# Where a slot's fill products stand: first half filled up to a third of the phase in place of a quarter

## The chip, the core and the metric

The kernel runs on one core of one Trainium2 chip. Times are device microseconds (us) of that core, from the start to the end of one execution. TensorE (PE, matmuls and their weight loads), VectorE (DVE), ScalarE (ACT), GpSimd (POOL) and SyncE (SP, which issues the DMAs here) each work through their own instructions in order and wait for each other through semaphores. Matmuls write to PSUM banks; ACT and DVE read them from there.

## What is computed

The reference works on 2048 tokens of 512 channels. `x` is layer-normed to `xn`. Branch A is causal attention with a window of 256 keys and 32 heads of 16 channels; branch B layer-norms `xn` again, and applies a two-layer MLP of 1792 hidden channels with tanh-GELU. The result is

```
s = attention(xn @ wqkv, window 256) @ wo        # 32 heads of 16
g = silu(gelu(layernorm(xn) @ w1 + b1) @ w2 + b2)
out = x + s * g
```

The kernel splits each float32 operand into a high and a low part and adds three matmuls (high·high, high·low, low·high) where the reference has one product.

## The kernel before, in words

**Stages.** A first stage loads and normalises `x` and projects the first heads (to about 62 us). The attention stage runs to about 447 us. The rest (447 to 764 us) is the MLP and the output projection.

**The attention stage** goes through 128 blocks, t = 0 to 127: eight groups n of four heads, with 16 blocks of 128 keys each. Within a group the heads are handled as two pairs, p = 1 and p = 0. One block, in the order in which PE gets its work (the loop is `for t in range(-16, end + 1)`, line 819):

1. `prob_block(p=1)` (line 548): two score matmuls into the tile `stb`, then an exponential on ACT from `stb` into a tile `pt`, then two mask operations on POOL.
2. `max_block` (line 496): four score matmuls into `xy` for the row maxima of the block 12 ahead (`LEAD`). DVE puts masked values from `zo` into `xy` (COPY_PREDICATED) and reduces `xy` to the maxima `mt` (TENSOR_REDUCE).
3. `fill_in(t, 0)` (line 812): the **first half's fill products**.
4. What `plan` holds for this block (casts, weight splits, DMAs).
5. `prob_block(p=0)`: again two score matmuls into `stb`, and the exponential. There is one `stb` tile, so these matmuls wait until the exponential of step 1 has read it; likewise step 1 of the next block waits for the exponential of this step.
6. `fill_in(t, 1)`: the **second half's fill products**.
7. `first_scores` (line 487): four matmuls into `zo` for the next block's maxima; they follow DVE's COPY_PREDICATED, which reads `zo`.
8. `pv_step` (line 569): up to 24 small matmuls of `pt` with the values `vt` into another part of `zo`, which ACT copies to `oraw`.

For t from 116 on there are no maxima left, and step 1 writes to `xy` instead of `stb`.

**The fill products** are work of other stages that is put between the attention's matmuls: query/key projections of later heads (`pair_qk`, 12 products to a phase), value projections (`pair_v`, 24), and hidden layers of the MLP (`pair_h`, 12). `tandem(t0, t1, one, two)` (line 440) makes two of them at once: each unit is a pair of matmuls on the lower and the upper 64 rows of the array, writing to the two banks `fb`. It has two phases (in the second, the operands change rows), n units each. `places` deals the n units of a phase over the blocks (slots) of that phase in even shares, and then splits each block's share between the first and the second half of the block; `ahead` (line 455) is the number in the first half. The second phase keeps up to `most` = n // 4 units for the first half of block t1. At t1 the two banks are copied out, one by ACT and one by DVE; then the high part is cast on ACT, the low part subtracted on POOL, and both are sent by DMA into the slots from which later blocks read queries and keys.

All instructions but the DMAs of an early part keep the order in which the program issues them.

Of the kernel before, what the change touches and what calls it, by code (L numbers as in the profile page):

```python
# [50 lines left out]
def mixer_kernel(ctx, tc, x, wqk, wv, wo, w1, b1, w2, b2, out):  # L51
# [25 lines left out]
    def load(pool, tag, src, name, shape=(P, 512)):  # L77
        t = pool.tile(list(shape), F32, tag=tag, name=name)
        nc.sync.dma_start(t, src)
        return t  # L80
# [359 lines left out]
    def tandem(t0, t1, one, two, mid=None, back=None):  # L440

        n = one[0]
        lo, hi = slice(0, 64), slice(64, P)
        mid = mid or max(1, (t0 + t1 + 1) // 2)
        most = n // 4

        def places(slots, last):

            last = min(most, n // (len(slots) + 1)) if last else 0
            cuts = [(n - last) * k // len(slots) for k in range(len(slots) + 1)]
            out = []
            for t, a, b in zip(slots, cuts, cuts[1:]):
                ahead = min(b - a, max(most, (b - a + 1) // 2))
                out += [(t, 0)] * ahead + [(t, 1)] * (b - a - ahead)
            return out + [(t1, 0)] * last

        first, second = places(range(t0, mid), False), places(range(back or mid, t1), True)
        for phase, where in enumerate((first, second)):  # L460
            for i in range(n):
                flags = dict(start=(phase == 0 and i == 0), stop=(phase == 1 and i == n - 1), skip_group_check=True)
                def unit(i=i, phase=phase, flags=flags):
                    made = ((two if phase == 0 else one)[1](fb[1 - phase], i, hi, **flags),
                            (one if phase == 0 else two)[1](fb[phase], i, lo, **flags))
                    if phase == 1 and i == 0:
                        for r in made:
                            tc.add_manual_dep(r.ins, outs["copy"].ins.name, ORDER, reason="the banks change rows")
                fills.setdefault(where[i], []).append((unit, ()))
        fills.setdefault((t1, int(t1 in BEHIND)), []).append((one[2], (fb[0], t1, nc.scalar.copy)))  # L470
        fills[t1, 0].append((two[2], (fb[1], t1, nc.vector.tensor_copy)))
# [203 lines left out]
    ahead = load(pp, "pt", x[512: 640, :], "x_1_0")  # L675
# [28 lines left out]
    n, raw = raws["qk"]  # L704
# [600 lines left out]
```

## Time and profile before

| | us |
|---|---|
| median of 3 runs | 765.21 (765.13 to 765.72) |
| the profiled execution | 765.6 |
| its span, first to last instruction | 763.9 |
| blocks 0 to 115 of the attention stage | 62 to about 409 |
| blocks 116 to 127 and the end of that stage | about 409 to 447 |
| MLP and output projection | 447 to 764 |

The profile is of one execution. The 1.7 us between its time and its span lie outside the first and last instruction. In a timeline view a row is a run of equal instructions: start, length of the run, engine, operation, output<-inputs, shape, count, and in brackets the idle time before the first one with what ended it. Matmul ends are modelled, so a matmul row can reach over the start of the next; the starts are what is compared below. PEld are weight loads, which run beside the matmuls.

### The profile page before, as it was taken

To read this page: it belongs to the slowest core of one execution; us is meant where nothing else is said; L and a number is where in the kernel's file an instruction comes from. 1 tells how busy PE (TensorE), PEld (TensorE's weight loads), DVE (VectorE), ACT (ScalarE), POOL (GpSimd) and SP (SyncE) were. 2 spreads that over 40 slices of the span, in tenths; PEclk is the share of its full clock that TensorE was granted. 3 is DMA by queue.
4 is the path that set the end of the run, shared out by engine and by line. 5 is a ranking of instruction groups with operands and counts; after the bars stand their busy time and mean duration, and the time that the engine had idled before them with its cause. 6 is when DMAs were issued, how large, how long until landed. Compare 5 with 4: busy or idle time off the path is not lost.

```text
span 763.9 us, 18757 instructions
## 1 busy us (share of the span) xinstructions
PE 748.9 (98%) x7408; PEld 587.6 (77%) x7408; DVE 511.2 (67%) x781; ACT 440.3 (58%) x746; POOL 300.4 (39%) x644
## 2 busy tenths in 40 slices
PE   8999999999999999999999999999999999999997
PEld 7886766777778887677776678888888888888886
DVE  7886766767766677887764447764657675676743
ACT  7756766767666666777877755444645553442001
POOL 6414657767566554867776800030101100001102
PEclk9999999999999999999999999999999999999999
DMA  8633345756555535555644283541202322244611
GB/s 282 187 78 83 79 121 145 195 148 185 140 136 137 136 87 156 134 153 132 173 153 152 61 276 129 186 156 42 83 28 89 104 85 85 80 150 133 215 54 55
DMA packets 56951, 99.40 MB, mean 130 GB/s; under 512 B 11104, under 2 KB 11360, under 8 KB 56864
## 3 DMA queue, kind: packets, MB, share of 16 engines
q1 hardware_dynamic: 56864, 98.21, 44.9%
q8 instruction: 58, 0.95, 0.5%
q14 instruction: 29, 0.24, 0.1%
HBM read 51.39 MB, written 29.62 MB: 106 GB/s over the span
## 4 chain that ended last, share of the span: by engine, by line
PE 87%; ACT 5%; DVE 3%; DMA 2%; issue 2%; POOL 0%; SPq 0%; ACTq 0%; DVEq 0%
PE acc L43 20%; PE fb L43 16%; PE zo L43 13%; PE stb L43 10%; PE p L43 9%; PE s L43 6%; PE h L43 6%; ACT pt L43 4%; PE xy L43 4%; PE pv L43 3%; DMA qk<-qk 2%; DVE xy L43 1%; PE yt L43 1%; DMA x<-in_x_dram 1%; DVE mt L43 1%
## 5 line engine op out<-in xcount | busy, mean ns | idle before, releaser
L43 POOL TENSOR_SCALAR_AFFINE_SELECT pt<-pt 128x256 f32<-128x256 f32 x480 | 194.8, 430 | 146.1 <-ACT pt L43 144.7
L43 ACT ACTIVATE pt<-stb 128x768 f32<-128x768 f32 (+1 forms) x244 | 188.6, 773 | 50.4 <-PE stb L43 39.6
L43 DVE TENSOR_REDUCE mt<-xy 128x4 f32<-128x1024 f32 (+1 forms) x128 | 152.6, 1192 | 4.4
L43 DVE COPY_PREDICATED xy<-upper,zo 128x512 f32<-128x512 int32 x112 | 77.9, 695 | 84.4 <-PE xy L43 77.1
L43 PE MATMUL fb<-xnT,wqb 64*128 64x512 f32 (+1 forms) x684 | 112.9, 398 | 0.2
L43 PE MATMUL stb<-qk 64*128 64x384 f32 (+1 forms) x488 | 103.1, 418 | 4.4 <-ACT pt L43 1.1
L43 POOL TENSOR_TENSOR xo<-xo,gated 128x512 f32<-128x512 f32 x15 | 20.3, 1356 | 216.6 <-DVE gated L43 213.1
L43 PE MATMUL zo<-pt,vt 128*17 128x128 f32 x2880 | 103.7, 275 | 0.1
L43 PE MATMUL acc<-w,gh 128*128 128x512 f32 x320 | 98.9, 390 | 0.0
L43 PEld LDWEIGHTS stb<-qk 64*128 64x128 f32 x488 | 45.5, 183 | 68.7 <-ACT pt L43 57.7
L43 PEld LDWEIGHTS zo<-pt,vt 128*17 128x17 f32 x2880 | 67.5, 97 | 15.7 <-issue 7.0
L43 PEld LDWEIGHTS fb<-xnT,wqb 64*128 64x128 f32 (+1 forms) x684 | 63.8, 185 | 7.8 <-DVE pjr L43 1.1
L43 PEld LDWEIGHTS acc<-w,gh 128*128 128x128 f32 x320 | 59.8, 188 | 12.1
L43 ACT COPY oraw<-zo 128x128 f32<-128x128 f32 x128 | 34.3, 268 | 56.7 <-PE zo L43 53.5
L43 PE MATMUL acc<-w,gl 128*128 128x512 f32 x160 | 62.4, 390 | 0.0
L43 PE MATMUL xy<-qk 64*128 64x256 f32 (+2 forms) x536 | 58.0, 290 | 0.3 <-DVE mt L43 0.2
L43 PEld LDWEIGHTS xy<-qk 64*128 64x128 f32 x536 | 47.0, 185 | 6.4 <-issue 2.8
L43 ACT ACTIVATE gated<-acc 128x512 f32<-128x512 f32 x16 | 8.7, 596 | 64.5 <-DVE acc L43 64.5
L43 PEld LDWEIGHTS zo<-qk 64*128 64x128 f32 x448 | 39.2, 185 | 7.8 <-issue 1.4
L43 PE MATMUL s<-wos,ohl 128*128 128x512 f32 (+1 forms) x204 | 44.7, 377 | 0.0
L43 PEld LDWEIGHTS s<-wos,ohl 128*128 128x128 f32 x204 | 36.6, 188 | 7.0
L43 ACT COPY p<-p 128x512 f32<-128x512 f32 x21 | 12.3, 585 | 49.5 <-PE p L43 42.0
(195 smaller groups left out, 1245.1 us busy)
## 6 DMA issues: line engine op xcount, KB each, us to landing
qk<-sh SPq DMA_DIRECT2D x128, 128.0 KB
qk<-pjr SPq DMA_DIRECT2D x64, 128.0 KB
oT_d<-oraw SPq DMA_DIRECT2D x32, 256.0 KB
w_d<-in_w_dram SPq DMA_DIRECT2D x14, 512.0 KB
x<-in_x_dram SPq DMA_DIRECT2D x16, 256.0 KB
or<-oT_d SPq DMA_DIRECT2D x16, 256.0 KB
w<-rden_d SPq DMA_DIRECT2D x16, 256.0 KB
xo<-in_x_dram SPq DMA_DIRECT2D x16, 256.0 KB
```

The lines of the kernel that those rows point to most:

```text
L43: r = issue(*args, **kwargs)
```

## The change

One line of `places` changes. In each block of a tandem phase, the number of units in the first half was the larger of a quarter of the phase and half of the block's share, and is now the larger of a third of the phase and half of the share, never more than the share.

```diff
@@ tandem, places
             for t, a, b in zip(slots, cuts, cuts[1:]):
-                ahead = min(b - a, max(most, (b - a + 1) // 2))
+                ahead = min(b - a, max(n // 3, (b - a + 1) // 2))
                 out += [(t, 0)] * ahead + [(t, 1)] * (b - a - ahead)
             return out + [(t1, 0)] * last
```

With n = 12 the first half holds up to 4 units in place of 3, and with n = 24 up to 8 in place of 6. Shares are 4, 5 or 6 units with n = 12 and 8, 9 or 12 with n = 24, so (first half, second half) goes from (3, 1), (3, 2), (3, 3) to (4, 0), (4, 1), (4, 2), and from (6, 2), (6, 3), (6, 6) to (8, 0), (8, 1), (8, 4). That is 99 blocks, of which 91 lie before t = 116; each moves one unit with n = 12 and two with n = 24, 116 units in all. The number `last` of units at t1 still follows `most` and stays. A moved unit now stands before the second score matmuls of its block on PE, where it stood after them; no instruction is added or removed, and the order of the other engines' instructions and of the DMAs stays.

## Prediction

> **What bounds the kernel now.** I read the page's busy times first, then the stretches, then the table of waits, then PE's own timeline in single blocks.
>
> ```profile
> PE 748.9 (98%) x7408; PEld 587.6 (77%) x7408; DVE 511.2 (67%) x781; ACT 440.3 (58%) x746; POOL 300.4 (39%) x644
> ```
> ```profile
> 62.19:408.00 345.81, 339.88 (x5027) 250.49 (x5028) 250.89 (x312) 243.35 (x418) 225.58 (x521) 1.00 0.54 138
> 447.00:764.00 317.00, 312.29 (x1413) 258.96 (x1411) 194.46 (x350) 126.11 (x209) 26.13 (x20) 1.00 0.34 112
> ```
> ```profile
> PEld stb L43 <- ACT pt L43: 57.7, 172, 0.5
> ```
>
> The second fence has stretches: length, then busy time of PE, PEld, DVE, ACT and POOL, then granted clock, DMA share and GB/s. In the changed stage (62 to 408 us) PE counts as busy for 339.9 of 345.8 us, so 5.9 us of idle at most. The waits tell more: weight loads for `stb` stood 172 times, 57.7 us in all, until ACT's exponential had read `stb`. A row of matmuls has modelled ends, so a hole in front of a waiting matmul can be covered by the row before it. Starts can't hide it.
>
> ```profile
> 187.37 0.44 PE L43 MATMUL stb<-qk 64*128 64x384 f32 x2
> 187.65 0.40 PE L43 MATMUL xy<-qk 64*128 64x256 f32 x4
> 187.89 0.87 PE L43 MATMUL fb<-xnT,wqb 64*128 64x512 f32 x6
> 188.80 0.44 PE L43 MATMUL stb<-qk 64*128 64x384 f32 x2
> 189.08 0.33 PE L43 MATMUL zo<-qk 64*128 64x128 f32 x4
> ...
> 190.15 0.44 PE L43 MATMUL stb<-qk 64*128 64x384 f32 x2
> 190.43 0.40 PE L43 MATMUL xy<-qk 64*128 64x256 f32 x4
> 190.76 0.97 PE L43 MATMUL fb<-xnT,wqb 64*128 64x512 f32 x6
> ...
> 193.14 0.44 PE L43 MATMUL stb<-qk 64*128 64x384 f32 x2
> 193.42 0.40 PE L43 MATMUL xy<-qk 64*128 64x256 f32 x4
> 193.65 0.87 PE L43 MATMUL fb<-xnT,wqb 64*128 64x512 f32 x6
> 194.57 0.44 PE L43 MATMUL stb<-qk 64*128 64x384 f32 x2
> 194.85 0.40 PE L43 MATMUL fb<-xnT,wqb 64*128 64x512 f32 x2
> 195.09 0.33 PE L43 MATMUL zo<-qk 64*128 64x128 f32 x4
> ...
> 196.13 0.45 PE L43 MATMUL stb<-qk 64*128 64x384 f32 x2
> ```
> ```profile
> 202.54 0.86 PE L43 MATMUL fb<-xnT,wqb 64*128 64x512 f32 x6
> 203.24 0.39 PE L43 MATMUL stb<-qk 64*128 64x256 f32 x2
> ```
> ```profile
> 187.94 0.81 ACT L43 ACTIVATE pt<-stb 128x768 f32<-128x768 f32 x1 [0.16 <-PE stb L43]
> 189.29 0.81 ACT L43 ACTIVATE pt<-stb 128x768 f32<-128x768 f32 x1 [0.54 <-PE stb L43]
> ```
>
> The block at 193.14 is a usual (3, 1) block. A pair costs 0.23 (194.85 to 195.09). From `stb` to `stb` its first half should last 0.28 + 0.23 + three pairs: in a block near a group's end, where the exponential is short, three pairs pass in 0.70 (202.54 to 203.24), so 1.21. It lasts 1.43 (193.14 to 194.57), as the three pairs take 0.92. **There is a hole of 0.22 us in the first half.** ACT's rows say why: the exponential starts 0.57 after its matmuls (187.37 to 187.94), takes 0.81, and the next `stb` follows 0.05 later. The second half has the same chain, a little shorter (0.49 + 0.81 + 0.05 = 1.35): the block at 187.37 is a t1 block (3, 0), and its second half lasts just that (188.80 to 190.15). With one pair in it a second half lasts 1.56 (194.57 to 196.13): there PE is the bound, by 0.21.
>
> So a block's time is the longer of PE and the exponential's chain, in each half apart; now the first half waits for ACT and the second works PE beyond it.
>
> [...] Read by busy time, 5.9 us is all there is to win here.
>
> **The change, part by part.** Nothing is added or taken away; PE's order alone changes, by 116 pairs in 99 blocks. What a move is worth depends on the block; I went through the starts of all 91 changed blocks before t = 116 (the first at 71.89, the last at 406.25):
>
> ```profile
> 71.89 0.44 PE L43 MATMUL stb<-qk 64*128 64x384 f32 x2
> ```
> ```profile
> 406.25 0.45 PE L43 MATMUL stb<-qk 64*128 64x384 f32 x2 [0.16 <-ACT pt L43]
> ```
>
> For each I took: new first half = old + 0.23 a moved pair (0.118 for a value pair) − the hole in its pairs' time; new second half = old − the same, but not under the chain's 1.35.
>
> - *47 blocks of 512-wide pairs with a full effect.* In (3, 1) the fourth pair fills the hole: 0.28 + 0.23 + 0.92 = 1.43 to 1.44, and the second half falls from 1.56 to 1.35. (3, 2) and (3, 3) keep pairs in the second half and save the whole 0.23. Gains of 0.17 to 0.23, 0.203 on average: **−9.56 us**.
> - *11 value blocks with a full effect.* Twelve matmuls take 0.91 (232.20 to 233.11), six without a hole 0.36 (233.39 to 233.75), so 0.12 a pair and a hole of 0.20. Eight pairs take 0.94; two pairs leave the second half: 0.195 each, **−2.14 us**.
>
> ```profile
> 232.20 0.92 PE L43 MATMUL fb<-wva,xnT 64*128 64x256 f32 x12
> 233.11 0.44 PE L43 MATMUL stb<-qk 64*128 64x384 f32 x2
> 233.39 0.52 PE L43 MATMUL fb<-wva,xnT 64*128 64x256 f32 x6
> 233.75 0.34 PE L43 MATMUL zo<-qk 64*128 64x128 f32 x4
> ```
>
> - *14 blocks with half an effect.* After a t1 block the first pair waits for DVE's copy of the bank (190.43 to 190.76 is 0.33, not 0.23), so part of the hole is before the pairs; or the second half soon meets 1.35; or the block follows a group's end. **−1.42 us** (0.10 each).
> - *19 blocks with none.* Near a group's end the exponentials are short and no hole is there (202.54 to 203.24): the pair costs in one half what it saves in the other. In a group's first blocks `pv_step` is short, and the second half stands at the chain already, pair or no pair:
>
> ```profile
> 212.01 0.45 PE L43 MATMUL stb<-qk 64*128 64x384 f32 x2
> 212.29 0.40 PE L43 MATMUL fb<-xnT,wqb 64*128 64x512 f32 x2
> ...
> 213.35 0.44 PE L43 MATMUL stb<-qk 64*128 64x384 f32 x2 [0.16 <-ACT pt L43]
> ```
>
> There the fourth pair saves nothing (212.01 to 213.35 is 1.34 with a pair inside) and costs up to 0.1: **+0.38 us**.
>
> - *8 blocks from t = 116 on*: maxima are done, `xy` and `stb` alternate, and the pairs run without a hole; moving one changes nothing: 0. Bounds: a gain of 0.2 each would need a hole that isn't there, a loss the same, ±1.6.
>
> Sum of the blocks: −9.56 − 2.14 − 1.42 + 0.38 = −12.74.
>
> **What comes back.** *A DMA.* In block 11 PE stood for the DMAs that bring in a chunk of queries and keys of the second group:
>
> ```profile
> 93.47 1.18 SPq L43 DMA_DIRECT2D qk<-pjr  x2
> ```
> ```profile
> 98.47 0.44 PE L43 MATMUL zo<-qk 64*128 64x128 f32 x4 [0.83 <-DVE mt L43]
> ```
>
> The profile names DVE, whose reduce was over before; the matmul that is held is the first to read that chunk, whose second transfer was issued at about 94.05, 4.4 us before. Blocks 9 to 11 (0.6 us of gain) lie between the sending and the need: they only lengthen that stall. +0.6. *DVE.* COPY_PREDICATED frees `zo` for `first_scores`; in a (4, 0) block that point is 0.2 earlier.
>
> ```profile
> 188.15 0.70 DVE L43 COPY_PREDICATED xy<-upper,zo 128x512 f32<-128x512 int32 x1 [1.14 <-PE xy L43]
> 188.88 1.23 DVE L43 TENSOR_REDUCE mt<-xy 128x4 f32<-128x1024 f32 x1
> ```
>
> In the (3, 0) block it ends at 188.85, and `first_scores` starts at 189.08: 0.23 to spare, and 0.3 for the next `xy` after the reduce. Blocks where DVE also normalises `y` (81 to 88) use that up: 1.08 for one such step in block 85. I take +0.25, between 0 and the whole gain of the 14 full-effect blocks with 2.6 us or more of DVE work (−0.2 × 14: +2.8).
>
> ```profile
> 322.25 1.08 DVE L43 TENSOR_SCALAR y<-y,mvC,rsC 128x512 f32<-128x512 f32 x1
> ```
>
> *ACT*'s casts stand between the two exponentials and end before the second (nothing late in the rows above), and POOL's masks are wanted only at the end of the next block: nothing.
>
> **Forecast: −12.74 + 0.85 = −11.9 us.** The profiled 765.6 (span 763.9) would become 753.7; against the median of 765.21, **753.3 us**.
>
> **The rivals.**
>
> - *A, new waits eat a part.* DVE in the 14 blocks above, or late chunks for other groups as in block 11. For: DMA share 0.54 and DVE 250.9 of what would be 334 us. Against: the spare 0.23 and 0.3. Price: +2.8 to +3.5, 756.5 us.
> - *B, busy time is true*: PE has 5.9 us to give in the stage. Against: three pairs at 0.92 here and 0.70 there. 765.2 − 5.9 = 759.3 us.
> - *C, it does nothing*: the hole moves with the pair, since the exponential starts later when the pairs before it are more. Against: the exponential of the first half is issued ahead of the pairs, and starts 0.57 after its own matmuls. 765.2 us.
> [...]
>
> [...]
>
> **How the numbers follow.** Forecast 0.74, A 0.13, B 0.04, C 0.04, D 0.05. The low end is the sum without what comes back, and with a fourth pair that costs the first half nothing (0.02 in 58 blocks): 765.2 − 12.74 − 1.2 = 751.3. The high end takes A in and adds the loss of ±1.6 from t = 116 on, rounded: 758. A change of over 0.2% (1.5 us), about what a measurement of this kernel can tell from none, is faster in the forecast, A and B: 0.91; same is C: 0.04; slower is D: 0.05.
>
> **What would show it.** In the changed profile a usual block should read: `stb` to second `stb` 1.43 to 1.45 with eight `fb` matmuls between, second `stb` to next `stb` 1.35, and a block 2.78 to 2.80 in place of 2.98. The wait of weight loads for `stb` on ACT should fall by a quarter or so from 57.7 us; the stall before `zo` in block 11 should grow by some 0.6. The stage from t = 0 to t = 116 should shorten by 12 us, and the MLP keep its 317. It is wrong if the second half stays over 1.45 with no pair in it (something else holds `stb`), if the first half grows to over 1.5, or if the rows before `zo` or `xy` start waiting for DVE.

## The result, and the profile after

The changed kernel takes 752.25 us (median of 4 runs, 751.99 to 752.90) against 765.47 us for the kernel before beside it: ratio 0.9827, 95% interval 0.9810 to 0.9844, 13.2 us less. The forecast was 753.3 us, from 751.3 to 758.0. The profiled execution takes 751.99 us, with a span of 750.3 us. Three executions in the experiments below were far slower than the others of their kernel (1383.05, 876.28 and 812.15 us), and the ratios leave them out.

The stretch from block 0 to block 115 and the stretch of the MLP, in the view of stretches (length, then busy time of PE, PEld, DVE, ACT, POOL; granted clock, DMA share, GB/s):

```profile
61.96:395.60 333.64, 327.75 (x5051) 252.62 (x5050) 251.78 (x312) 243.34 (x419) 225.42 (x523) 1.00 0.56 144
433.80:750.30 316.50, 311.88 (x1411) 258.74 (x1409) 194.78 (x350) 126.06 (x209) 26.11 (x20) 1.00 0.35 112
```

The attention stretch went from 347.0 us (62.19 to 409.23) to 333.6 us (61.96 to 395.60); the MLP kept its 316.5. PE's idle time in the attention stretch, by the rows quoted here and in the prediction, was 345.81 − 339.88 = 5.9 us before and is 333.64 − 327.75 = 5.9 us after. **All of the 13 us came out of time that the page counts as PE busy.** The wait that shrank is in the table of waits; the first row is of the kernel before, the other two of the changed one:

```profile
ACT pt L43 <- PE stb L43: 39.6, 99, 0.7
```
```profile
PEld stb L43 <- ACT pt L43: 45.1, 161, 0.7
ACT pt L43 <- PE stb L43: 51.7, 139, 0.8
```

Weight loads for `stb` waited 57.7 us for ACT before, 45.1 us now. The wait the other way round, of ACT's exponential for PE, grew from 39.6 us to 51.7. The starts tell which half is held by what: where the exponential holds it, the next `stb` starts some 0.05 us after its end. Within 0.08 us of that end start the second `stb` of 104 of the 116 first halves before and of 43 after, and the next block's `stb` behind 20 of 115 second halves before and 66 after. So the change took the exponential's wait out of the first halves, and brought many second halves down to it.

PE's timeline of the blocks that the prediction showed (t = 41 to 43, now from 182.20 on; the first row below is the second `stb` of block 41):

```profile
183.63 0.45 PE L43 MATMUL stb<-qk 64*128 64x384 f32 x2
183.91 0.33 PE L43 MATMUL zo<-qk 64*128 64x128 f32 x4
184.18 0.85 PE L43 MATMUL zo<-pt,vt 128*17 128x128 f32 x24
184.98 0.45 PE L43 MATMUL stb<-qk 64*128 64x384 f32 x2
185.27 0.40 PE L43 MATMUL xy<-qk 64*128 64x256 f32 x4
185.58 1.19 PE L43 MATMUL fb<-xnT,wqb 64*128 64x512 f32 x8
186.61 0.33 PE L43 MATMUL stb<-qk 64*128 64x384 f32 x2
186.78 0.33 PE L43 MATMUL zo<-qk 64*128 64x128 f32 x4
187.05 0.85 PE L43 MATMUL zo<-pt,vt 128*17 128x128 f32 x24
187.85 0.45 PE L43 MATMUL stb<-qk 64*128 64x384 f32 x2
188.13 0.40 PE L43 MATMUL xy<-qk 64*128 64x256 f32 x4
188.37 1.11 PE L43 MATMUL fb<-xnT,wqb 64*128 64x512 f32 x8
189.30 0.43 PE L43 MATMUL stb<-qk 64*128 64x384 f32 x2
189.57 0.38 PE L43 MATMUL zo<-qk 64*128 64x128 f32 x4
189.87 0.85 PE L43 MATMUL zo<-pt,vt 128*17 128x128 f32 x24
190.65 0.44 PE L43 MATMUL stb<-qk 64*128 64x384 f32 x2
```

Block 43 (from 187.85): its first half lasts 1.45 with four pairs in it (before: 1.43 with three), its second half 1.35 with none (before: 1.56 with one), together 2.80 against 2.99. Four pairs take 0.93, which is 0.23 each: the hole is full. Block 42 is the first after a t1 block: its first pair starts 0.31 after `xy` (185.27 to 185.58), held by DVE's copy of the bank, and so it gains half as much (2.87 against 2.99).

Block by block, the four groups of the prediction against the starts in the two traces:

| group | blocks | worked out | measured |
|---|---|---|---|
| 512-wide pairs, full effect | 47 | −9.56 | −9.82 |
| value pairs, full effect | 11 | −2.14 | −2.55 |
| half effect | 14 | −1.42 | −1.07 |
| none | 19 | +0.38 | −0.16 |
| blocks not changed | 24 | 0 | +0.19 |

The sum is −13.4 us; the rest of the kernel is the same to 0.2 us. Of the +0.19 in blocks that were not changed, 0.15 is block 84 (below).

### The profile page after: what moved, and what is told of

It is laid out like the page before. It is cut to its first block, busy times and chain, and to the rows that moved or that the text cites. A ratio compares the mean times of both kernels' runs of the same rounds, so it can differ in the third digit from the quotient of the medians.

```text
span 750.3 us, 18757 instructions
## 1 busy us (share of the span) xinstructions
PE 735.8 (98%) x7408; PEld 589.3 (79%) x7408; DVE 511.3 (68%) x781; ACT 439.5 (59%) x746; POOL 299.1 (40%) x644
## 4 chain that ended last, share of the span: by engine, by line
PE 90%; ACT 4%; DVE 3%; DMA 1%; issue 1%; POOL 0%; SPq 0%; DVEq 0%; ACTq 0%
PE acc L43 20%; PE fb L43 19%; PE zo L43 12%; PE stb L43 9%; PE p L43 9%; PE s L43 6%; PE h L43 6%; PE xy L43 5%; PE pv L43 3%; ACT pt L43 3%; DVE xy L43 1%; PE yt L43 1%; DVE mt L43 1%; DMA qk<-pjr 0%; DMA x<-in_x_dram 0%
## 5 line engine op out<-in xcount | busy, mean ns | idle before, releaser
L43 ACT ACTIVATE pt<-stb 128x768 f32<-128x768 f32 (+1 forms) x244 | 188.4, 772 | 58.4 <-PE stb L43 51.7
L43 PE MATMUL fb<-xnT,wqb 64*128 64x512 f32 (+1 forms) x684 | 106.9, 398 | 0.3
L43 PE MATMUL stb<-qk 64*128 64x384 f32 (+1 forms) x488 | 98.9, 401 | 4.5 <-ACT pt L43 2.8
L43 PEld LDWEIGHTS stb<-qk 64*128 64x128 f32 x488 | 45.5, 183 | 53.3 <-ACT pt L43 45.1
L43 PEld LDWEIGHTS s<-wos,ohl 128*128 128x128 f32 x204 | 36.7, 188 | 7.0
```

Source lines behind the costliest of these rows:

```text
L43: r = issue(*args, **kwargs)
```

## The experiments

The theory: each half of a block takes the longer of PE's work and the chain matmul, exponential, next matmul on the one `stb` tile; the change fills a hole of about 0.2 us. The rivals: the order as such is worth something per moved pair; the blocks help each other through DMAs and DVE; PE held the first half all along. A diff with a + alone shows the line that stands in place of the changed line of `places`.

**The two kinds of phase, one at a time.**

```diff
-ahead = min(b - a, max(n // 3, (b - a + 1) // 2))
+ahead = min(b - a, max(n // 3 if n == 12 else most, (b - a + 1) // 2))
```

> A third of the phase only where a phase has 12 pairs (queries, keys, hidden layers); the value phases keep 6 of 24. Theory (each half of a block is the longer of PE's work and the exponential's chain; the change fills the hole of the first half): the parts add up, since each block stands for itself. In the two traces blocks 54 to 74 became 3.1 us shorter and the others 10.3 us, so this run should take 752.3 + 3.1 = 755.3 us. Rival (the gain comes through what the blocks hand on to each other, DMAs and DVE's backlog): the two parts don't add up, and this run is off 755.3 by over 1.5 us.

Measured: 755.39 us (754.79 to 755.69), ratio 0.9876 (0.9862 to 0.9889).

```diff
+ahead = min(b - a, max(n // 3 if n == 24 else most, (b - a + 1) // 2))
```

> A third only in the value phases (8 of 24); phases of 12 keep 3. Theory of the hole: 765.4 - 3.1 = 762.3 us. Rival (the parts depend on each other): off by over 1.5 us, and its loss against before doesn't make up the sum with the other part.

Measured: 762.08 us (761.53 to 762.52), ratio 0.9963 (0.9949 to 0.9976); the kernel before beside both took 764.73. Against it the two parts save 9.3 and 2.7 us, together 12.0; the whole change took 13.2 us off 765.47, and 12.8 off 765.03 in a later run. The parts add up within their intervals of about 1 us, as they should if the blocks stand for themselves.

**Fewer pairs in the first half.**

```diff
+ahead = min(b - a, n // 6)
```

> First halves hold 2 of 12 and 4 of 24, the rest of a share goes to the second half. Theory of the hole: the first half stays at 1.41 to 1.43 us with two pairs, since the exponential sets it, and each pair that goes over lengthens the second half by its 0.23 (0.118 for a value pair): 58 blocks with 0.23 each (13.4 us), 9 and 6 more with the same (3.5), none where the second half has 0.2 to spare or the exponential is short: 765.4 + 16.9 = 782 us. Rival (the first half was held by PE, not by the exponential): it shortens by 0.23 and the time stays at 765.

Measured: 783.02 us (one run). Block 43 of this kernel, in PE's timeline:

```profile
198.03 0.44 PE L43 MATMUL stb<-qk 64*128 64x384 f32 x2
198.31 0.40 PE L43 MATMUL xy<-qk 64*128 64x256 f32 x4
198.55 0.63 PE L43 MATMUL fb<-xnT,wqb 64*128 64x512 f32 x4
199.47 0.44 PE L43 MATMUL stb<-qk 64*128 64x384 f32 x2 [0.28 <-ACT pt L43]
199.75 0.62 PE L43 MATMUL fb<-xnT,wqb 64*128 64x512 f32 x4
200.20 0.33 PE L43 MATMUL zo<-qk 64*128 64x128 f32 x4
```

With two pairs the first half lasts 1.44 (198.03 to 199.47), as with three and with four. Here the hole is so wide that the modelled end of the pairs (198.55 + 0.63) leaves 0.28 of idle in front of the second `stb`, and the profile names the exponential. The same waits in this run: 68.5 us of weight loads for `stb` on ACT. Of the 116 first halves in this run, 108 end within 0.08 us of the exponential's end. It was the exponential that held the first half, and not PE.

**More pairs in the first half.**

```diff
+ahead = min(b - a, max(5 * n // 12, (b - a + 1) // 2))
```

> First halves hold up to 5 of 12 and 10 of 24: 54 more pairs are moved, in blocks with shares of 5, 6, 9 and 12. Theory of the hole: the hole is full with 4, so a fifth lengthens the first half by what it takes from the second: 752.3 us within 1.0. Usual blocks then read first half 1.67, second half 1.25 to 1.33 for a share of 5. Rival (a pair is cheaper ahead of the second score matmuls whatever stands there; 13.2 us for 116 pairs is 0.114 each): 752.3 - 54 x 0.114 = 746 us.

Measured: 752.40 us, ratio 0.9835 (0.9822 to 0.9849). One more execution, for its trace:

> Up to 5 of 12 and 10 of 24 in the first half, for its trace: 752.4 us as before; a block with a share of 5 reads first half 1.67 and second half 1.25 to 1.33 by the theory of the hole (together 2.92 to 3.00, as with 4 and 1), and 1.67 and 1.10 by the rival that a pair is cheaper there.

Measured: 752.30 us. Block 40, which has a share of 5, first in the changed kernel, then here:

```profile
179.22 0.45 PE L43 MATMUL stb<-qk 64*128 64x384 f32 x2
179.50 0.40 PE L43 MATMUL xy<-qk 64*128 64x256 f32 x4
179.74 1.10 PE L43 MATMUL fb<-xnT,wqb 64*128 64x512 f32 x8
180.68 0.41 PE L43 MATMUL stb<-qk 64*128 64x384 f32 x2
180.93 0.39 PE L43 MATMUL fb<-xnT,wqb 64*128 64x512 f32 x2
181.16 0.33 PE L43 MATMUL zo<-qk 64*128 64x128 f32 x4
...
182.20 0.44 PE L43 MATMUL stb<-qk 64*128 64x384 f32 x2
```
```profile
179.15 0.44 PE L43 MATMUL stb<-qk 64*128 64x384 f32 x2
179.44 0.40 PE L43 MATMUL xy<-qk 64*128 64x256 f32 x4
179.67 1.32 PE L43 MATMUL fb<-xnT,wqb 64*128 64x512 f32 x10
180.83 0.33 PE L43 MATMUL stb<-qk 64*128 64x384 f32 x2
181.00 0.33 PE L43 MATMUL zo<-qk 64*128 64x128 f32 x4
...
182.06 0.45 PE L43 MATMUL stb<-qk 64*128 64x384 f32 x2
```

With (4, 1) the halves last 1.46 and 1.52, with (5, 0) 1.68 and 1.23: 2.98 and 2.91. In this block the fifth pair adds 0.22 us to the first half and takes 0.29 from the second. In others of the 42 blocks before t = 116 where one or two pairs more were moved the balance is the other way (block 52 grows by 0.19); over all 42 it is +0.25 us, and the whole run is the same. A worth per moved pair (746 us) is out.

**The blocks without a hole alone.**

```diff
+NONE = (46, 48, 62, 78, 94, 95, 3, 4, 17, 33, 36, 49, 50, 51, 82, 97, 99, 100, 113, *range(116, 128))
+ahead = min(b - a, max(n // 3 if t in NONE else most, (b - a + 1) // 2))
```

> The change in the 27 blocks alone in which the prediction found no gain (19 before t = 116 without a hole or with the second half at the exponential's chain already, and the 8 from t = 116 on). Theory of the hole: nothing, 765.0 us as before, within 0.5. Rival (each moved pair is worth the same 0.114): 28 pairs, 3.2 us faster, 761.8.

Measured: 765.22 us against 765.03, ratio 1.0001 (0.9992 to 1.0010). The 28 pairs moved in these 27 blocks are worth nothing, as worked out block by block; at 0.114 us a pair it would have been 761.8 us.

**The cause made smaller.** Both kernels leave out the third key block of each window (256 columns in place of 384 in `prob_block`, two key blocks in place of three in `pv_step`), and with it the second mask operation. This makes the exponential shorter (585 ns on average in place of 773, in the first of the two against the kernel before), and PE's and POOL's work too (1984 value matmuls in place of 2880, and 256 mask operations in place of 480):

```diff
@@ prob_block
-        w = min(384, S - P * kb)
+        w = min(256, S - P * kb)
@@ pv_step
-        lo = max(qb - 2, 0)
+        lo = max(qb - 1, 0)
```

> The kernel before with its cause shortened: scores, exponential and values take 256 columns in place of 384, so the third key block of each window is left out of the attention; the exponential falls from 0.81 to about 0.60 us. Theory of the hole: first half with three pairs 0.22 + 0.235 + 0.70 = 1.16 on PE against 0.51 + 0.60 + 0.05 = 1.16 of the exponential, so no hole; a block of 2.99 becomes about 2.45, and the time about 715 us (estimate, 705 to 725). What counts is the difference to the next run.

> The changed kernel with the same third key block left out. Theory of the hole: there is no hole to fill, so the change is worth nothing here: 0 to 4 us slower than the run before (0.07 in 58 blocks where the second half comes to the exponential's chain of 1.08). Rival (the order itself is worth the 0.114 us a pair, hole or not): 13 us faster than the run before.

Measured: 727.51 us with the order before, 726.32 us with the changed one; ratios 0.9513 (0.9499 to 0.9528) and 0.9501 (0.9486 to 0.9517), which overlap. Here the change is worth 1.2 us by the medians, of its 13, and not clearly anything: in the traces, 1.05 us of the difference falls in one block, t = 110. The time of 715 us for the first of the two was an estimate and missed by 12 us. PE's and DVE's rows of block 45 in the first of them say why:

```profile
184.86 0.50 PE L43 MATMUL xy<-qk 64*128 64x256 f32 x4
187.14 0.38 PE L43 MATMUL stb<-qk 64*128 64x256 f32 x2
```
```profile
185.46 0.69 DVE L43 COPY_PREDICATED xy<-upper,zo 128x512 f32<-128x512 int32 x1 [0.54 <-PE xy L43]
186.19 1.23 DVE L43 TENSOR_REDUCE mt<-xy 128x4 f32<-128x1024 f32 x1
```

PE's `xy` of that block starts at 184.86 and DVE ends at 187.42, 2.56 later; the next block starts at 187.14 and its `xy` 0.33 on, when DVE has just let go. The loop through `xy` sets the block at 2.61 us there, not the exponential and not PE. In 59 of 102 blocks of this kernel, and in 60 of the other, `xy` starts within 0.08 us of the end of DVE's reduce; in the kernel before and in the changed one it does so in none. So in these two kernels the hole was gone (in block 45 the three pairs of the first take 0.69 us, 185.20 to 185.89, and the four of the second 0.94, 185.03 to 185.97), but a wait for DVE had come in its place, which could have eaten a gain from PE's order too. They agree with the theory but don't prove it: that a moved pair is worth nothing without a hole is shown by the kernel above, with the change in the 27 blocks alone.

**The hole of t1.** Blocks t1 have three pairs and a hole that the change leaves:

```diff
@@ tandem
-        most = n // 4
+        most = n // 3
```

> Built on the changed kernel: the number kept for block t1 follows a third too (4 of 12, 8 of 24), so the last slot of a second phase has 4 in place of 5 (8 in place of 9), and t1 has 4 (8) in its first half. Theory of the hole: t1 blocks in the changed kernel are (3, 0) with a hole of about 0.2, so the fourth pair is free there, and 10 slots of 5 save 0.22, three value phases 0.24: -2.9 us. But ACT's copy of the bank at t1 waits for the last pair, and where it stands ahead of the second exponential (t1 = 8, 53, 68, 84, 98, 115) it makes that one late by about 0.3: +1.8. So 752.3 - 1.1 = 751.2 us. Rival (the hole of t1 is needed by the copies everywhere): no gain, 752.3 or above.

The second kernel has this as well:

```diff
-    BEHIND = (19, 24, 35, 41, 58, 74, 90, 104)
+    BEHIND = (8, 19, 24, 35, 41, 53, 58, 68, 74, 84, 90, 98, 104, 115)
```

> As the run before, with t1 = 8, 53, 68, 84, 98 and 115 added to the blocks where ACT's copy of the bank stands in the second half, behind the second exponential. Theory of the hole: the late exponentials go, 752.3 - 2.9 = 749.4 us. Rival (the copy costs the same wherever it stands): 751.2, no better than the run before.

Measured: 750.72 us, ratio 0.9814 (0.9799 to 0.9829), and 750.18 us, 0.9808 (0.9793 to 0.9823). The second was expected at 749.4 and, if the copy's place made no difference, at 751.2; its time lies between, and the two intervals overlap. The traces tell more. Between the two traces the second halves of blocks 8, 53, 68, 84 and 98 fall by 0.20 to 0.30 each (1.55 to 1.34 in block 8), as the theory of the late exponential has it. But the copy behind the exponential can hold up the next block's first exponential: block 9 grows by 0.44, 54 and 99 by 0.12 and 0.14, while 69 and 85 stay as they were. Of the 1.21 us that the moved copies save, 0.70 is given back one block later. (Block 56 grows by 0.28 too, but in this one trace alone.) Without t1 = 8 in the list, and with the changed kernel on the same chip:

> The changed kernel unaltered, beside the next runs on one chip: 752.3 us by every theory. In its trace the three blocks 9 to 11 should last about 9.5 us, with the held matmul of block 11 some 3.7 to 4.4 us after the last transfer was issued, if the transfer's own time varies from one execution to the next.

> As the run with the copies of t1 behind the second exponential, but with t1 = 8 left as in the kernel before: there the copy behind the exponential made the next block's first half 0.44 us longer (1.44 to 1.88) for 0.23 saved. Theory of the hole: 750.2 - 0.2 = 750.0 us, and 2 us under the changed kernel beside it. Rival (t1's free half is worth nothing, and the two runs before were a better chip): no difference to the changed kernel beside it.

Measured: the changed kernel 752.28 us, ratio 0.9834 (0.9821 to 0.9847); the extended one **750.13 us**, 0.9805 (0.9792 to 0.9818). The intervals don't overlap: the pair in the hole of t1, together with the copies moved in five t1 blocks, is worth 2.1 us, and this version beats both kernels. Its block 41, a t1 block, in PE's timeline:

```profile
181.51 0.44 PE L43 MATMUL stb<-qk 64*128 64x384 f32 x2
181.79 0.40 PE L43 MATMUL xy<-qk 64*128 64x256 f32 x4
182.03 1.09 PE L43 MATMUL fb<-xnT,wqb 64*128 64x512 f32 x8
182.95 0.44 PE L43 MATMUL stb<-qk 64*128 64x384 f32 x2
```

The first half lasts 1.44 with four pairs (182.20 to 183.63 in the changed kernel: 1.43 with three).

## Why the prediction was right, and where it was off

- *The bound*: right. The hole was there, it was the exponential's, and matmul rows hid it. With two, three and four pairs the first half of a usual block lasts 1.44, 1.43 and 1.45 us, and with five 1.68: four fill it. PE's busy share of the span is 98% before (748.9 of 763.9 us) and after (735.8 of 750.3) and tells nothing of the gain; the weight loads' share of the stretch rose from 72% (250.49 of 345.81) to 76% (252.62 of 333.64).
- *The terms of the sum*: −12.74 worked out, −13.6 measured in the changed blocks. The full groups gained 0.7 us more than worked out. That it is no more is partly luck, as two errors work against each other: block by block, by the prediction's rule, the first halves of these 58 blocks came out about 1.3 us longer than worked out and the second halves about 1.9 us shorter. The rule missed that a second half whose `stb` needn't wait is cheaper (last section): it gets under the 1.35 that I took as its floor (186.61 to 187.85 in block 42 is 1.24), and it loses more than the price of its pairs (in value block 55 from 2.05 to 1.75, where two pairs were put at 0.236). The group without an effect gained 0.16 us where a loss of 0.38 was worked out, and the half group gained 0.35 less.
- *8 blocks from t = 116 on*: right, and the run with the blocks without a hole, which has these 8 too, took no less time; from the last `stb` of block 115 to the first `acc` of the MLP it is 36.7 us before and 36.8 after.
- *What comes back*: this is the step that was furthest off for its size. It was put at +0.85 on top of the changed blocks' sum; the −13.6 already holds what came back in the changed blocks, and the others add +0.19. Two terms:

  - *The DMA of block 11 (+0.6)*: half right. The stall before `zo` was to grow by 0.6; the idle time in the profile's bracket went from 0.83 to 0.72. Blocks 9 to 11 last 10.25 us in the profile before, 9.50 after, 0.75 less and not the same. But 10.25 was a long sample: in the run with value phases alone, which differs from the kernel before from block 54 on only, they last 9.69 (the transfer released PE after 3.86 us in place of 4.42), and in the one with the blocks without a hole, where these three stand as before, 9.88. Where they are changed the same way they last 9.50, 9.50 and 9.53, and in the t1 experiments 9.58 and 9.66, and 9.95 where block 9 grew by 0.44. Without the long sample some 0.2 of the 0.6 was gained, and whether the rest came back can't be told: the transfer's own time moves by more than the effect. Here are the sending and the held matmul in the changed kernel; the profile now names the DMA where it had named DVE:

```profile
92.66 1.17 SPq L43 DMA_DIRECT2D qk<-pjr  x2
```
```profile
96.91 0.44 PE L43 MATMUL zo<-qk 64*128 64x128 f32 x4 [0.72 <-DMA qk<-pjr]
```

  - *DVE in blocks 81 to 88 (+0.25)*: wrong in place. The changed blocks there with a hole gained 0.18 to 0.24 each, as worked out. DVE did hold PE in block 29, where the subtraction of a weight split (1.33 us) of block 28 pushes COPY_PREDICATED to 1.30 us after the block's start in place of 1.08, and `first_scores` waits for it (0.28 us of idle before its weight load, ended by DVE); that block gained 0.06 in place of 0.22:

```profile
147.32 1.33 DVE L43 TENSOR_TENSOR wqb<-wqkr,wqb 128x512 fp32r<-128x512 f32 x1
148.58 0.20 DVE L43 STREAM_TRANSPOSE mT<-mh 128x32 f32<-128x32 f32 x1
148.71 0.66 DVE L43 COPY_PREDICATED xy<-upper,zo 128x512 f32<-128x512 int32 x1
```

- *ACT and POOL, put at nothing*: nearly. Block 84 is a t1 block and was not changed, but its second half lasts 1.50 in place of 1.34. Its `xy` starts 0.39 after the block's start in place of 0.29, and its pairs 0.64 in place of 0.46. ACT's copy of the bank waits for the last of them and stands ahead of the second exponential, which so starts 0.62 after its matmuls (0.48 before) and holds the next `stb`:

```profile
307.84 0.58 ACT L43 COPY pjr<-fb 128x512 f32<-128x512 f32 x1 [0.20 <-PE fb L43]
308.32 0.82 ACT L43 ACTIVATE pt<-stb 128x768 f32<-128x768 f32 x1
309.19 0.45 PE L43 MATMUL stb<-qk 64*128 64x384 f32 x2 [0.27 <-ACT pt L43]
```

  POOL's masks are not what holds it: `pv_step` starts 1.81 after the block's start in both kernels. Why `xy` is late stays open.
- *Rival A* was so much: blocks 29, 84 and 107, about 0.5 us together, not 2.8. In the second profile of the changed kernel 29 and 84 read the same within 0.01, but block 107 gains 0.19 like the others: its late `first_scores` (by 0.17) belongs to the one execution. *B* is out by the size of the gain. *C* is out by the time, and by the exponential of block 43, which starts 0.57 after its matmuls with four pairs behind it (187.85 to 188.42) as with three. *D*, the 0.05 for a slower kernel, is out by the 13.2 us gained. That a PE with fewer holes is granted a lower clock, no run here shows: it is 0.999 or 1.00 in the four runs of the changed kernel, and 0.999 in the profile of the kernel before.

## What to carry to other kernels

When an engine is said to be 98% busy, compare starts: a stretch of equal matmuls that takes 0.92 us in one place and 0.70 in another hides a wait of 0.22. Work that has to be put somewhere belongs into such holes up to the point where the two chains of that half are equal; beyond it a moved piece costs what it saves (two pairs 783 us, three 765, four 752, five 752). Sort the places first by which chain ends last in each; in this kernel that told, before any run, 58 blocks that gained 0.2 us on average from 27 that gained next to nothing.

## What the runs showed that was not expected

- A half that doesn't wait for `stb` is cheaper by up to 0.11 us than one that does. When the first half's pairs run past the end of the exponential, the weights for the second `stb` are loaded beside the pairs (at 186.41 in block 42), and the next matmuls follow 0.17 after its start (186.61 to 186.78) in place of 0.28 (183.63 to 183.91). The exponential, too, starts 0.38 after it in place of 0.49. These are ACT's rows of the same two halves of the changed kernel:

```profile
184.12 0.81 ACT L43 ACTIVATE pt<-stb 128x768 f32<-128x768 f32 x1 [0.54 <-PE stb L43]
186.99 0.81 ACT L43 ACTIVATE pt<-stb 128x768 f32<-128x768 f32 x1 [0.63 <-PE stb L43]
```

- The same transfer of 128 KB, issued at the same point of the program, released the PE that waited for it between 3.67 and 4.42 us after its issue, in ten profiles with the full attention window. In the two with the short window PE came for it 2.44 and 2.46 us after the issue and did not have to wait, so there it had landed by then. What sets its time stays open.
